# Weight loads behind a GpSimd gate, a second queue for the first small rows, and a mask in four selections, in a fused attention and tanh-shrink MLP kernel

## The chip, the cores and the metric

The kernel runs on one core of a Trainium2 chip. The metric is the time of one execution on the device in microseconds (us). Of the kernel before, three timed executions are given (median 357.6 us, 356.88 to 357.86) and one profiled execution, from which every duration below is taken.

## The reference

For 8 batches of 8 heads (sequence 576, head size 64) two attentions are added: a full one over q, k and v averaged in groups of four positions, whose result is repeated four times, and a local one in which a position sees only the positions less than four away. The sum, with the heads side by side, is x of 4608 tokens by 512. The output is (h - tanh(h)) @ w_out with h = x @ w_in.

```python
q_d, k_d, v_d = (t.reshape(B, H, Sd, 4, D).mean(axis=3) for t in (q, k, v))
out_up = np.repeat(sm_attn(q_d, k_d, v_d), 4, axis=2)
mask = np.abs(pos[:, None] - pos[None, :]) < 4
out_local = softmax(where(mask, scale * q @ k.T, -1e9)) @ v
x = (out_up + out_local).transpose(0, 2, 1, 3).reshape(B * S, H * D)
h = x @ w_in                       # 4608x512 @ 512x2048
out = (h - np.tanh(h)) @ w_out     # 4608x2048 @ 2048x512
```

## The kernel before

**The work.** Attention goes by pairs of heads: 32 pairs, four to a batch. Pair p belongs to batch p // 4, and its place in the batch is j = p % 4. Its inputs are K and Q rows (tile `st`, two transfers of 256 KB, L305), V rows (tile `vst`, two transfers of 160 KB, L329, the second holding the second head) and, once per batch, the last rows of K and Q that do not fit in 128 partitions (tile `sr`, four transfers of 64 KB, L318). K and Q are cast (L430, small rows L422), transposed on TensorE in the first 12 pairs (L453, L440) and copied back (L456, L444, L480, L485/L486 for the K side). Scores are L518, L526 and L532, exponentials L537, L541 and L545, the mask multiply L559. V is cast to `vw` (L360), its pooled form is a TensorE product (L391) copied out at L396. L572 multiplies the exponentials with V, L587 and L589 normalise, L614/L615 transpose back, L619 copies one piece, and L607 (`join`) writes the pair's 128 rows of `xT`.

**The dense part.** Tokens go in 9 blocks of 512. `mm1` (L645) multiplies `w_in` with `xT` into 16 pieces of 128 features, L658 takes the tanh, L661 the difference into `gT`; `mm2` (L671) multiplies `gT` with `w_out`; L685 copies and L696 stores. Block 0 needs the four pairs of batch 0, block 1 those of batches 0 and 1. Piece fc of `mm1` reads part fc // 4 of `w_in`; `mm2` goes through the four parts of `w_out` in turn for each 128 tokens.

**The weights.** Both matrices are loaded once, in four parts each, by DMAs that GpSimd issues (`load_w`, L345 and L349) and that cast float32 to bf16: 512 KB written for each part. They lie in a queue of their own; all other loads are issued by SyncE.

**The order.** No engine picks its work at run time. A planner (`Plan.order`, L58) goes through the operations with a cost and a priority for each, gives every engine the operation that can start first and, among those that could, the one of the lowest `pri`, and writes out one fixed order for each engine. An engine then works through its order and waits wherever an operand is not there. DMA is planned as one further lane, in which the transfers of all queues follow each other: 1000 ns for 256 KB of K or Q, 940 ns for 160 KB of V, 3100 ns for a part of the weights. Where the planned order leaves TensorE a gap of over 350 ns before the first `mm1` of block 1, `emit` writes matmuls on a zero tile into three quarters of it (`filler`, L799, L801 in the profile). The planner lets a weight load be issued once the *issue* of some V load has been planned (`("q", after)`); on the chip nothing makes it wait.

**Start.** GpSimd fills the constants (`c_mask` L284 with ten selections at L291 and L294), clears two tiles `v4` for later pairs (L744) and then reaches the weight loads. SyncE issues the small rows of batch 0 first, then K, Q and V pair by pair.

Of the kernel before, what the change touches and what calls it, by code (L numbers as in the profile page):

```python
# [7 lines left out]
FP32 = mybir.dt.float32  # L8
# [6 lines left out]
class Plan:  # L15
# [3 lines left out]

    LAT = {"PE": 270, "ACT": 160, "DVE": 130, "POOL": 160, "SP": 50, "DMA": 1900}

    def __init__(self):
        self.ops = []
# [32 lines left out]
    def order(self):  # L58
        ops, n = self.ops, len(self.ops)
        users = [[] for _ in range(n)]  # L60
        left = [0] * n
        for i, o in enumerate(ops):
            left[i] = len(o["deps"])
            for d in o["deps"]:
                users[d].append(i)
        at = [o["after"] for o in ops]
        free, ready = {}, {}
        start, engine = [None] * n, [None] * n
        pending = {k: len(v) for k, v in self.users.items()}
        ends = {}  # L70
        bank_free = [0.0] * 8
        held = [None] * 8
        port_free = 0.0
        self.held = []

        def make_ready(i):
            for eng in ops[i]["alts"]:
                ready.setdefault(eng, []).append(i)

        def bank_time(i):  # L80
            o = ops[i]["opens"]
            if not o:
                return 0.0, None
            best = (float("inf"), None)
            for c in o[1]:
                if any(held[b] is not None for b in c):
                    continue
                t = max(bank_free[b] for b in c)
                if t < best[0]:
                    best = (t, c)  # L90
            return best
        for i in range(n):
            if left[i] == 0:
                make_ready(i)
        for _ in range(n):
            best = None
            for eng, cand in ready.items():
                if not cand:
                    continue
                fr = free.get(eng, 0.0)  # L100
                if eng == "DMA":
                    i = min(cand, key=lambda i: (at[i], i))
                    now = max(fr, at[i])
                else:
                    now, i = None, None
                    eff = []
                    for c in cand:
                        t = max(at[c], bank_time(c)[0], fr)
                        if ops[c]["alts"][eng][3]:
                            t = max(t, port_free)  # L110
                        eff.append((t, c))
                    now = min(eff)[0]
                    if now == float("inf"):
                        continue
                    i = min((ops[c]["pri"], c) for t, c in eff if t <= now)[1]
                if best is None or now < best[0]:
                    best = (now, eng, i)
            if best is None:
                raise RuntimeError(f"no operation can be put next: {[(e, [(ops[c].get('what'), at[c], ops[c]['opens']) for c in cs[:6]]) for e, cs in ready.items()]} {held}")
            now, eng, i = best  # L120
            for other in ops[i]["alts"]:
                ready[other].remove(i)
            o = ops[i]
            _, ns, fn, port = o["alts"][eng]
            o["fn"], o["ns"] = fn, ns
            if o["opens"]:
                name = o["opens"][0]
                c = bank_time(i)[1]
                self.place[name] = c
                for b in c:  # L130
                    held[b] = name
                self.held.append([name, c, now, None])
            start[i], engine[i] = now, eng
            end = now + ns
            free[eng] = end
            if port:
                port_free = end
            for name in o["names"]:
                ends[name] = max(ends.get(name, 0.0), end + self.LAT[eng])
                pending[name] -= 1  # L140
                if pending[name] == 0:
                    for b in self.place[name]:
                        held[b] = None
                        bank_free[b] = ends[name]
                    for h in self.held:
                        if h[0] == name:
                            h[3] = ends[name]
            for u in users[i]:
                same = eng in ops[u]["alts"] and len(ops[u]["alts"]) == 1 and eng != "DMA"
                at[u] = max(at[u], end if same else end + self.LAT[eng] + ops[u]["slack"])  # L150
                left[u] -= 1
                if left[u] == 0:
                    make_ready(u)
        self.start, self.engine = start, engine
        return sorted(range(n), key=lambda i: (start[i], i))
# [22 lines left out]
def kernel(  # L178
# [9 lines left out]
    nc = tc.nc  # L188
# [3 lines left out]
    NP = H // 2  # L192
# [6 lines left out]
    STEP = 112  # L199
# [17 lines left out]
    def fixed(name, shape, dt, n=None, pool=const):  # L217
        if n is None:
            return pool.tile(shape, dt, name=name, tag=name)
        return [pool.tile(shape, dt, name=f"{name}{i}", tag=f"{name}{i}")  # L220
                for i in range(n)]

    NST, NVST, NVW, NV4 = 4, 5, 4, 2
    ident = fixed("ident", [128, 128], BF16)
    group = fixed("group", [128, 32], BF16)
    pick = fixed("pick", [128, 6, 128], BF16)
# [56 lines left out]

    def c_mask():  # L284
        GP.memset(mask, 1.0)
        parts = []
        for t in range(NT):
            parts.append((mask[:, COL[t]:COL[t] + 4 * NG[t]].rearrange(
                "p (c g) -> p c g", c=4), NG[t], STEP * t - 4 * G0[t]))
        for part, n, d in parts:  # L290
            GP.affine_select(  # L291
                out=part, in_=part, compare_op=ALU.is_ge, fill=0.0,
                base=d + 3, pattern=[[-1, 4], [-4, n]], channel_multiplier=1)
            GP.affine_select(  # L294
                out=part, in_=part, compare_op=ALU.is_ge, fill=0.0,
                base=3 - d, pattern=[[1, 4], [4, n]], channel_multiplier=-1)

    def load(ns, fn, keys, cost, pri, after=0.0):
        op("SP", ns, fn, writes=list(keys) + [("q", keys[0])], pri=pri, after=after)
        op("DMA", cost, None, reads=[("q", keys[0])], writes=keys, pri=pri)  # L300

    def load_qk(p):
# [7 lines left out]
    def load_rest(b):  # L310

        s = b % 2
        for n, src in enumerate((k, q)):
            for hh in range(2):
                base = src[b, hh]

                def issue(n=n, hh=hh, base=base):
                    nc.sync.dma_start(out=sr[s][n::2, hh, :], in_=bass.AP(  # L318
                        tensor=base.tensor, offset=base.offset + 512 * D,
                        ap=[[4 * D, 16], [2 * S * D, NP], [1, 4 * D]]))  # L320
                load(450, issue, [("sr", s, n, hh)], 260, 40 * b - 3000 - 4)

    def load_v(p):
        b, j, s = p // NP, p % NP, p % NVST
# [17 lines left out]
    def load_w(src, dst, name, f, after):  # L342
        def issue():
            if src is moe_w_in:
                GP.dma_start(out=dst[:, :, 512 * f:512 * f + 512],  # L345
                             in_=src[:, 512 * f:512 * f + 512].rearrange(
                                 "(c p) f -> p c f", p=128))
            else:
                GP.dma_start(out=dst[:, 4 * f:4 * f + 4, :],  # L349
                             in_=src.rearrange("(f p) n -> p f n", p=128)  # L350
                             [:, 4 * f:4 * f + 4, :])
        op("POOL", 1000, issue, reads=[("q", after)],
           writes=[(name, f), ("wq", name, f)], pri=-5000)
        op("DMA", 3100, None, reads=[("wq", name, f)], writes=[(name, f)], pri=-30)

    def prep_v(p):
        s, w = p % NVST, p % NVW
# [384 lines left out]
           pri=-9940)  # L742
    for i in range(NV4):
        op("POOL", 900, lambda i=i: GP.memset(v4[i], 0.0),  # L744
           writes=[("v4", i, 0), ("v4", i, 1)], pri=-20, port=True)

    load_qk(0)
    load_rest(0)
# [2 lines left out]
            load_qk(p + 1)  # L751
        load_v(p)
    for f in range(4):
        load_w(moe_w_in, w_in_sb, "w_in", f, ("vst", (2 + f) % NVST if f < 2 else 3, 1))
    nl = [NP]

    def load_next():
        if nl[0] < NPAIR:
            if nl[0] % NP == 0:
                load_rest(nl[0] // NP)  # L760
            load_qk(nl[0])
            load_v(nl[0])
            nl[0] += 1
        if 0 <= nl[0] - NP - 1 < 4:
            load_w(moe_w_out, w_out_sb, "w_out", nl[0] - NP - 1,
                   ("vst", (nl[0] - 1) % NVST, 1))

    work = [attention(p) for p in range(NPAIR)]
    for a in work:
# [63 lines left out]
```

## Time and profile before

| | |
|---|---|
| median of 3 executions | 357.6 us (356.88 to 357.86) |
| profiled execution: its own time | 358.21 us |
| profiled execution: span, first to last instruction | 356.5 us |
| mean granted TensorE clock | 0.966 |
| TensorE busy | 329.3 us (92%) |
| VectorE, ScalarE, GpSimd busy | 221.3, 225.2, 129.7 us |
| weights' queue (software dynamic) | 4224 packets, 4.19 MB |
| all other loads, stores, transposes (hardware dynamic) | 97824 packets, 50.61 MB |

The page gives busy time by engine over the span, then the span in 40 slices of 8.9 us with one digit per engine (tenths of the slice). A busy TensorE is not a TensorE at its best: filler matmuls count as busy, and the granted clock stands in a row of its own. The chain of waits is followed back from the last instruction; the timeline of one engine lists its instructions with the idle time ahead of them and what ended it. A DMA's issue (SPq, POOL) and its landing are two things: the issue is the time on the issuing engine.

### The profile page before, as it was taken

What the parts mean: (1) busy time and instruction counts of PE and PEld (TensorE: products, weight loads), DVE (VectorE), ACT (ScalarE), POOL (GpSimd) and SP (SyncE); (2) the same over time, 40 slices, a digit from 0 to 9 for tenths busy, and PEclk for the clock granted to TensorE, in tenths of its full rate; (3) what the DMA queues carried; (4) which work ended last, traced back from release to release, by engine and by line L of the source; (5) the groups of instructions that cost most, each with busy time, mean ns of one, the idle gap of its engine ahead of it and who ended that gap; (6) DMA issues with size and microseconds to landing.
All of it is one profiled execution on the core that took longest, in us unless ns stands there. A gap on an engine that the chain in (4) does not pass through costs nothing.

```text
span 356.5 us, 7044 instructions
## 1 busy us (share of the span) xinstructions
PE 329.3 (92%) x2574; PEld 169.1 (47%) x2621; DVE 221.3 (62%) x409; ACT 225.2 (63%) x396; POOL 129.7 (36%) x161
## 2 busy tenths in 40 slices
PE   5826699999999999999999999999999999999994
PEld 2414355555554544554454444545555444444441
DVE  3715378756897487868959875788686533444300
ACT  3525378666987477578967886898787344444411
POOL 8303323153433331744929557548441000000000
PEclk9855899999999999999999999999999999999999
DMA  5999997848998916999699978723510211111031
GB/s 155 239 208 222 263 254 217 225 112 185 243 242 203 262 46 149 212 265 266 154 239 253 223 207 230 190 71 94 121 31 2 59 30 33 40 48 31 29 88 60
DMA packets 102083, 55.26 MB, mean 155 GB/s; under 512 B 69152, under 2 KB 97440, under 8 KB 102048
## 3 DMA queue, kind: packets, MB, share of 16 engines
q1 hardware_dynamic: 97824, 50.61, 56.5%
q0 software_dynamic: 4224, 4.19, 7.0%
q8 instruction: 20, 0.33, 0.4%
q14 instruction: 15, 0.12, 0.1%
HBM read 43.65 MB, written 9.44 MB: 149 GB/s over the span
## 4 chain that ended last, share of the span: by engine, by line
PE 83%; issue 1%; ACT 1%; DVE 1%; ACTq 0%
PE ps L671 35%; PE ps L645 34%; PE ps L572 4%; PE ps L614 3%; PE ps L518 2%; PE ps L526 1%; PE ps L453 1%; PE ps L532 1%; PE ps L391 1%; PE ps L615 0%; ACT kt L485 0%; ACT kq L456 0%; ACT y L685 0%; DVE xT L607 0%; DVE half L495 0%
## 5 line engine op out<-in xcount | busy, mean ns | idle before, releaser
L645 PE MATMUL ps<-xT,w_in_sb 128*128 128x512 bf16 x552 | 140.3, 382 | 2.0 <-issue 0.6
L671 PE MATMUL ps<-w_out_sb,gT 128*128 128x512 bf16 x557 | 139.3, 379 | 1.5 <-issue 0.8
L661 DVE TENSOR_TENSOR gT<-ps,u 128x512 bf16<-128x512 f32 x144 | 97.7, 687 | 54.3 <-ACT u L658 52.6
L658 ACT ACTIVATE u<-ps 128x512 f32<-128x512 f32 x144 | 85.8, 599 | 48.8 <-PE ps L645 45.7
L645 PEld LDWEIGHTS <-w_in_sb 128*128 128x128 bf16 x576 | 53.0, 98 | 59.5 <-issue 1.8
L671 PEld LDWEIGHTS <-gT 128*128 128x128 bf16 x576 | 52.6, 98 | 56.5
L495 POOL TENSOR_TENSOR half<-kq 128x576 f32<-128x576 bf16 x22 | 29.9, 1358 | 41.1 <-DVE kq L480 20.5
L559 DVE TENSOR_TENSOR E<-E,mask 128x1152 bf16<-128x1152 bf16 x32 | 27.9, 871 | 18.8 <-ACT E L541 18.8
L537 ACT ACTIVATE E<-ps 128x912 bf16<-128x912 f32 x32 | 29.8, 932 | 8.8 <-PE ps L518 6.0
L685 ACT COPY y<-ps 128x512 f32<-128x512 f32 x36 | 21.1, 585 | 17.2 <-PE ps L671 17.0
L430 POOL CAST qr<-st 128x512 bf16<-128x512 f32 x37 | 24.1, 661 | 21.1 <-DMA st<-in_k_dram 17.3
L377 POOL TENSOR_TENSOR vp<-v 128x256 bf16<-128x256 f32 x20 | 14.6, 731 | 46.8 <-PE ps L572 46.4
L589 DVE TENSOR_TENSOR ln<-ps,r 128x768 bf16<-128x768 f32 x32 | 30.6, 956 | 1.1 <-DVE r L587 0.2
L485 ACT COPY kt<-kq 128x576 bf16<-128x576 bf16 x22 | 26.0, 1181 | 2.4 <-DVE kq L480 2.2
L373 POOL TENSOR_TENSOR v<-v 128x512 f32<-128x512 f32 x20 | 26.2, 1312 | 1.0
L572 PEld LDWEIGHTS <-E 128*128 128x128 bf16 x576 | 22.3, 99 | 8.1 <-DVE E L559 1.1
L360 ACT CAST vw<-vst 128x640 bf16<-128x640 f32 x21 | 15.3, 731 | 14.8 <-DMA vst<-in_v_dram 7.5
L607 DVE TENSOR_TENSOR xT<-ps,od 128x336 bf16<-128x336 bf16 x64 | 16.5, 300 | 12.1 <-ACT od L619 12.1
L545 ACT ACTIVATE E<-ps 128x576 bf16<-128x576 f32 x32 | 20.9, 653 | 0.0
L572 PE MATMUL ps<-vw,E 128*128 128x65 bf16 x320 | 19.5, 195 | 0.7 <-DVE E L559 0.5
L500 POOL TENSOR_TENSOR qkd<-half 128x288 bf16<-128x288 f32 x17 | 14.0, 825 | 16.3 <-PE ps L572 8.5
L572 PE MATMUL ps<-vp,E 128*128 128x65 bf16 x256 | 18.3, 195 | 0.0
(64 smaller groups left out, 264.0 us busy)
## 6 DMA issues: line engine op xcount, KB each, us to landing
vst<-in_v_dram SPq DMA_DIRECT2D x64, 160.0 KB, 4.1
st<-in_k_dram SPq DMA_DIRECT2D x32, 256.0 KB, 3.9
st<-in_q_dram SPq DMA_DIRECT2D x32, 256.0 KB, 4.0
v<-in_v_dram SPq DMA_DIRECT2D x20, 256.0 KB, 3.6
w_in_sb<-in_moe_w_in_dram POOLq DMA_DIRECT2D x4, 512.0 KB, 12.4
w_out_sb<-in_moe_w_out_dram POOLq DMA_DIRECT2D x4, 512.0 KB, 16.1
out_dram<-y SPq DMA_DIRECT2D x8, 256.0 KB, 3.1
out_dram<-y SPq DMA_DIRECT2D x8, 224.0 KB, 2.6
```

The costliest lines, as they stand in the source:

```text
L373: eng.tensor_tensor(out=v2, in0=v4[s][:, :, :, 0:128], in1=v4[s][:, :, :, 128:256], op=ALU.add)
L430: (eng, ns, lambda dst=dst, src=src, fn=fn: fn(out=dst, in_=src), port)
L485: ("ACT", 1180, lambda: A.copy(out=ktv, in_=src), False),
L495: eng.tensor_tensor(out=half, in0=flat[:, 0:576], in1=flat[:, 576:1152], op=ALU.add)
L537: A.activation(out=E[s][:, :, E0:E0 + 456], in_=at(s1)[:, :, PS0:512], func=AF.Exp, scale=SCALE)
L559: op("DVE", 760, lambda: V.tensor_tensor(out=el, in0=el, in1=mask.unsqueeze(1).to_broadcast([128, 2, S]), op=ALU.mult), reads=["mask"], wr ...
L572: T.matmul(po[:, hh, 65 * n:65 * n + 65], E[s][:, hh, e:e + 128], vv, start=start, stop=stop)
L589: op("DVE", 960, lambda: V.tensor_tensor(out=ln[s].rearrange("p n (h d) -> p h n d", d=D), in0=blocks()[:, :, :, 0:64], in1=r[s].unsqueeze ...
L645: T.matmul(at(name)[:, 0, :], w_in_sb[:, dc, fc * 128:(fc + 1) * 128], xT[dc][:, kb * 512:kb * 512 + 512], start=(dc == 0), stop=(dc == N_ ...
L658: op("ACT", 600, lambda: A.activation(out=u[us], in_=at(name)[:, 0, :], func=AF.Tanh), reads=[("hd", kb, fc)], writes=[("u", us)], pri=-1, ...
L661: op("DVE", 690, lambda: V.tensor_tensor(out=gT[g][:, fc, :], in0=at(name)[:, 0, :], in1=u[us], op=ALU.subtract), reads=[("hd", kb, fc), ( ...
L671: T.matmul(at(name)[:, 0, :], gT[g][:, fc, ts * 128:ts * 128 + 128], w_out_sb[:, fc, :], start=(fc == 0), stop=(fc == N_FF - 1))
```

## The change

Four things are edited.

1. **A gate ahead of the weights.** Before the first `w_in` part GpSimd copies one element of the second V tile of pair 2 (`vst[2]`) into a one-element tile `gate`. The copy can run only when that transfer has landed, and since GpSimd works in order, all eight weight loads are issued after it. The four `w_out` loads are queued together when pair 4 is loaded, not one for each pair. In the planner the weights get a DMA lane of their own, `DW`, with 6200 ns for a part, and a transfer of the other lane takes up to twice its cost while `DW` is occupied.
2. **Small rows of batch 0** are issued by ScalarE, not by SyncE.
3. **The mask** is made by four selections over three or two column groups at once, not by ten over one.
4. **The clearing of `v4`** gets priority 75 in the planner, not -20.

```diff
@@ Plan.order @@
-                if eng == "DMA":
+                if eng in ("DMA", "DW"):
...
+            if eng == "DMA":
+
+                ns += min(ns, max(0.0, free.get("DW", 0.0) - now))
             end = now + ns
@@ c_mask @@
-        for part, n, d in parts:
+        for part, n, m, d, e in (
+                (mask[:, 0:336].rearrange("p (t c g) -> p t c g", t=3, c=4), 3, 28, -8, 0),
+                (mask[:, 336:576].rearrange("p (t c g) -> p t c g", t=2, c=4), 2, 30, 0, -8)):
             GP.affine_select(
                 out=part, in_=part, compare_op=ALU.is_ge, fill=0.0,
-                base=d + 3, pattern=[[-1, 4], [-4, n]], channel_multiplier=1)
+                base=d + 3, pattern=[[e, n], [-1, 4], [-4, m]], channel_multiplier=1)
...
@@ load_rest @@
-                    nc.sync.dma_start(out=sr[s][n::2, hh, :], in_=bass.AP(
+                    (nc.scalar if b == 0 else nc.sync).dma_start(out=sr[s][n::2, hh, :], in_=bass.AP(
...
-                load(450, issue, [("sr", s, n, hh)], 260, 40 * b - 3000 - 4)
+                load(450, issue, [("sr", s, n, hh)], 260, 40 * b - 3000 - 4,
+                     eng="ACT" if b == 0 else "SP")
@@ load_w @@
-        op("POOL", 1000, issue, reads=[("q", after)],
-           writes=[(name, f), ("wq", name, f)], pri=-5000)
-        op("DMA", 3100, None, reads=[("wq", name, f)], writes=[(name, f)], pri=-30)
+        if after:
+            op("POOL", 110, lambda: GP.tensor_copy(out=gate, in_=vst[after[1]][0:1, 1, 4, 0:1]),
+               reads=[after], writes=["gate"], pri=-5001, port=True)
+        op("POOL", 760, issue, reads=["gate"], writes=[(name, f), ("wq", name, f)], pri=-5000)
+        op("DW", 6200, None, reads=[("wq", name, f)], writes=[(name, f)], pri=-30)
@@ start @@
         op("POOL", 900, lambda i=i: GP.memset(v4[i], 0.0),
-           writes=[("v4", i, 0), ("v4", i, 1)], pri=-20, port=True)
+           writes=[("v4", i, 0), ("v4", i, 1)], pri=75, port=True)
...
-        load_w(moe_w_in, w_in_sb, "w_in", f, ("vst", (2 + f) % NVST if f < 2 else 3, 1))
+        load_w(moe_w_in, w_in_sb, "w_in", f, ("vst", 2, 1) if f == 0 else None)
@@ load_next @@
-        if 0 <= nl[0] - NP - 1 < 4:
-            load_w(moe_w_out, w_out_sb, "w_out", nl[0] - NP - 1,
-                   ("vst", (nl[0] - 1) % NVST, 1))
+        if nl[0] == NP + 1:
+            for f in range(4):
+                load_w(moe_w_out, w_out_sb, "w_out", f, None)
```

## The prediction

> **What bounds the kernel now.** I read the page's slices first, then the chain of waits, then the timelines of the engines over the first 60 us, then the DMA queues by window.
>
> ```profile
> PE   5826699999999999999999999999999999999994
> PEclk9855899999999999999999999999999999999999
> DMA  5999997848998916999699978723510211111031
> ```
>
> From the sixth slice on (after some 46 us) TensorE is full. The windows view gives 295.95 us busy in 52 to 352 us, so 4 us idle in 300; what happens there can't give much. Ahead of that the slices are poor, the clock is at half, and DMA is full from the second slice on. The chain can be followed back no further than
>
> ```profile
> 487 pieces in order of time: start us, us, what
> ...
> 45.97 1.01 PE ps L645 x4
> ```
>
> so the last 310 us are TensorE's work one after the other, and the time is the moment at which the dense part starts in earnest, plus that. Up to 46 us an engine waits for a transfer: pair 2's V holds ScalarE and TensorE, pair 3's K and V hold GpSimd.
>
> ```profile
> 26.00 0.73 ACT L360 CAST vw<-vst 128x640 bf16<-128x640 f32 x1 [6.62 <-DMA vst<-in_v_dram]
> ...
> 26.78 0.80 PE L391 MATMUL ps<-vw,pick 128*128 128x128 bf16 x6 [6.21 <-ACT vw L360]
> ...
> 28.23 0.61 POOL L430 CAST qr<-st 128x512 bf16<-128x512 f32 x1 [15.77 <-DMA st<-in_k_dram]
> ...
> 38.21 0.72 POOL L360 CAST vw<-vst 128x640 bf16<-128x640 f32 x1 [6.64 <-DMA vst<-in_v_dram]
> ...
> 47.96 0.52 DVE L607 TENSOR_TENSOR xT<-ps,od 128x336 bf16<-128x336 bf16 x2 [1.01 <-ACT od L619]
> ```
>
> The last line is pair 3's `join`, which block 0 needs: 10.3 us from V landing (38.2) to its end (48.5). Why the V rows come late is in the issues and in the queues from 18 to 24 us:
>
> ```profile
> 7.49 3.13 POOL L345 DMA_DIRECT2D w_in_sb<-in_moe_w_in_dram  x4
> 10.59 1.87 POOL L349 DMA_DIRECT2D w_out_sb<-in_moe_w_out_dram  x2
> ...
> 9.56 1.42 SPq L329 DMA_DIRECT2D vst<-in_v_dram  x2
> ...
> q0 software_dynamic: 931, 0.93, 90.8%
> q1 hardware_dynamic: 929, 0.23, 29.7%
> ```
>
> Columns of the last two: packets, MB, share of 16 engines. The two queues pass as many packets (931 and 929), but a weight packet is 1 KB and a V packet 256 bytes: V gets 0.04 MB/us (0.23 MB in 6 us). Pair 2's second V transfer takes 15.7 us from issue to landing. The weights' queue is active from 10.1 to 41.5 us: 31.4 us, 3.9 us a part.
>
> **The change part by part.** *The gate.* Ahead of V of pair 2 lie 2.8 MB (three pairs of 832 KB, small rows 256 KB). Without weights the queues moved 289 GB/s in 5 to 10 us and 261 in 42 to 57 us: 10 to 11 us from the first data at 2.2 us, so V of pair 2 lands at 12 to 13.5 us instead of 25.9; I take 13. Behind it on the same queue are pair 3's K and Q (0.52 MB, 1.9 us: 15 instead of 28 and 30 us). The first weight packet came 2.6 us after its issue began (7.49 to 10.1), so weights run from 13 + 2.6 = 15.6 to 47 us. Of pair 3's 1280 V packets some 740 are through by then; the other 540 go at the weights' rate of 4224 packets in 31.4 us, 134 per us, and take 4 us: landed at 19.6 us instead of 38.2. With the measured 10.3 us to the `join`, and 2 to 3 us because pairs 0 to 3 now come close together on VectorE, `xT` of batch 0 is complete at 32 to 33 us instead of 48.5. `w_in` parts land at 3.9 us intervals from 19.5 to 31.3 us, in time; `w_out` is there by 47 us, and its first use (65.4 us now, some 50 after) still finds it. Cap of the gain: 15 us.
>
> The copy of one element has no row; the nearest are memsets of one element per partition (0.10 us) and the V cast (0.72 us): 0.1 taken. Queued behind the waiting copy on GpSimd are the eight issues and then casts and sums of pairs 3 and on. Today GpSimd waits from 12.5 to 28.2 us anyway, so the wait until 13 us costs nothing; were the cover gone, pair 3's cast would wait for the eight issues. These cost 8 x 0.82 us (3.13 + 1.87 us for six) = 6.6 us, to 19.6 us. More than six issues in one go are not shown: from nothing to waiting for the first part (19.5 us) and another; I take nothing, as the sixth took 1.1 us at most.
>
> The Trainium skill speaks against queueing them there: by "SBUF — State Buffer", sections "SBUF: two separate sides" and "A bandwidth-pool intuition that's wrong", VectorE's two-port operations keep GpSimd from writing descriptors, and a load of 0.62 us becomes one of 3.1 us. By the page the eight could take up to 25 us, an estimate, and the sum would lose most of its gain. The row says 0.75 to 1.13 us for the issues between 7.5 and 12.5 us, with VectorE busy in half of that time, and I go by it.
>
> *What becomes late next.* The weights are as many as before and now lie over batch 1. Packet for packet: small rows 256, then per pair 256 + 256 + 2 x 640 = 1792. To the end of V of pair 5 that is 540 + 256 + 3584 = 4380, at 134 per us 32.6 us: about 46 to 48 us, when the weights end; from rates by bytes (pair 3 with the second small rows, 14.6 us, and 12.2 us for a pair) 44 us. I take 46. Now it lands at 46.6 to 47.3 us, no later; but TensorE reaches its product (L391) only here:
>
> ```profile
> 59.26 0.52 PE L391 MATMUL ps<-vw,pick 128*128 128x128 bf16 x6
> ```
>
> With 0.7 us for the cast and 0.5 us to the product it can run at 47 us, 12.3 us earlier. How much of block 0 stands ahead of it in the new order is not in the trace. Before, it was 10 of 16 pieces of 0.86 us. If the planner leaves ten there too, the gain is 12.3 us; if none, 12.3 - 8.6 = 3.7 us. Its lanes make pair 5's V due some 7 us earlier than before (weights no longer in the same lane), so nearer the middle: five pieces, 12.3 - 4.3 = 8 us. Pairs 6 and 7 come after the weights at full rate, 3 us a pair, by 53 us, and TensorE has 13.8 us of `mm2` of block 0 for that time. From there on the order is as full as before, and the gain is kept.
>
> *ScalarE's issues.* The four small transfers took SyncE 1.33 + 1.23 us; all later loads go out 2.6 us sooner, which is in the 12 to 13.5 above (DMA was 21% busy in the first 5 us). No issue by ScalarE is shown; SyncE's and GpSimd's rows give 0.6 to 0.8 us, so 2.5 to 3 us in all, beside ScalarE's wait until 5.12 us; without that cover they'd cost 3 us once.
>
> *Mask and clearing.* Ten selections ran from 2.60 to 5.76 us, 3.2 us. Four of 336 and 240 columns: by the rows of 32 (0.21) and 120 columns (0.30) some 1 ns a column, 0.52 and 0.42 each, 1.9 us in all; bounds 1.2 and 3.2. The mask's first reader is at 15.17 us, and GpSimd then waits for the gate: nothing. The clearing (1.84 us) likely stays where it is, since GpSimd has nothing else ready; later it would cost 1.84 us on an engine that is busy 36% of the time: nothing.
>
> **Sum.** The profiled execution's own time is 358.2 us (span 356.5), 0.6 above the median. 358.2 - 8 = 350.2; less 0.6: **349.6 us**.
>
> **The rivals.** *A, the whole lead is kept* (15%): pair 5 stands behind enough of block 0, and only pair 3's lead counts: 13 to 15 us, 344. For it: V of pair 5 lands no later than today. Against it: an order written out in advance, with TensorE waiting at each place.
>
> *B, batch 1 takes the lead back* (19%): product of pair 5 ahead of nearly all of block 0, its V at 48 us or later, perhaps also pair 6's cast on ScalarE ahead of the tanh: gain below 4 us, 354 to 358.7, a third of it within the limit of measurement. For it: 0.04 MB/us for V under the weights. That the change does nothing is in here too: if V of pair 2 landed so late that the gate costs what it brings. Against it: the bytes in the queue ahead of it.
>
> *C, slower: the planner reckons the weights too dear* (16%). With 8 x 6200 ns = 49.6 us for what the chip did in 31.4 us, the last part of `w_out` is due near 67 us in the order and there near 48 us. Between the parts TensorE has 3.5 us of `mm2` for 6.2 us, so gaps of up to 2.7 us, into which `emit` writes filler matmuls that then have to be run, and attention is put ahead of `mm2`. Against: pairs 4 to 7 have about 8 us of TensorE work for these gaps. It ends slower than before once fillers and misplaced work cost over 8 us: 37 matmuls of 0.216 us on top of the 41 weight loads of L801 now. At 12 us: 361 us.
>
> **How the numbers follow.** The likeliest case (50%) is a gain of 4 to 12.5 us, 345 to 353.5 us, at 349.6. The range 342.5 to 359 takes in A's greater part and B, and leaves out C and the end of A, just under 2 in 10. A measurement of this kernel can tell about 0.3%, 1.1 us, from no change: faster 0.50 + 0.15 + 0.13 = 0.78, same 0.06, slower 0.16.
>
> **What would show it.** Right: V cast of pair 2 (L360) at 13 to 15 us with no wait of 6 us; eight weight issues in one row from about 13 us; the weights' queue active to about 47 us; pair 3's `join` (L607) at 32 to 34 us; the chain traceable to before 40 us; the product of pair 5 waiting for DMA to about 47 us, with `mm1` pieces ahead of it; 52 us and on as full as now. Wrong: weight issues of 2 us and more, GpSimd held after the sixth issue, the third V landing after 18 us, more than 60 filler matmuls after 30 us, or new idle time of TensorE beyond 60 us.

## The result and the profile after

| | before | after |
|---|---|---|
| median of 7 runs each, same chip | 357.72 us (356.88 to 358.43) | 355.65 us (354.5 to 356.34) |
| ratio, 95% interval | | 0.9941 (0.9921 to 0.996) |
| profiled execution: its own time, span | 358.21, 356.5 us | 356.3, 354.6 us |
| mean granted TensorE clock | 0.966 | 0.978 |

The change makes the kernel faster by 2.1 us, 0.6%. The forecast was 349.6 us, a gain of 8.

The page's slices of after; a slice is 8.9 us:

```profile
PE   6782679999999999989999999999999999999994
PEclk9997869999999999999999999999999999999998
DMA  8999998958959647999699987534401211111131
```

The DMA row is full from the second slice as before. TensorE does more in the third slice (8, before 2) and has its own hole now in the fourth and fifth (2 and 6), from 27 to 45 us, with the clock below full in the fourth to sixth (7, 8, 6). The chain of waits, first without a window and then in the window from 20 to 60 us:

```profile
473 pieces in order of time: start us, us, what
...
25.93 19.75 DMA vst<-in_v_dram
...
45.79 0.74 POOL vw L368
46.57 0.80 PE ps L399 x6
47.37 4.27 PE ps L653 x10
```

It can be followed into the transfer of pair 5's V, 19.75 us long, through its cast to its product on TensorE. (The line numbers are 8 higher than before in this region.) GpSimd's timeline shows the gate and both V casts:

```profile
13.42 0.31 POOL L359 COPY gate<-vst 1x1 f32<-1x1 f32 x1 [2.17 <-DMA vst<-in_v_dram]
13.68 3.15 POOL L351 DMA_DIRECT2D w_in_sb<-in_moe_w_in_dram  x4
16.80 3.20 POOL L355 DMA_DIRECT2D w_out_sb<-in_moe_w_out_dram  x4
...
33.10 0.72 POOL L368 CAST vw<-vst 128x640 bf16<-128x640 f32 x1 [10.55 <-DMA vst<-in_v_dram]
...
45.79 0.73 POOL L368 CAST vw<-vst 128x640 bf16<-128x640 f32 x1 [7.83 <-DMA vst<-in_v_dram]
```

The gate opens at 13.4 us and the eight issues go out back to back. V of pairs 4 (33.1) and 5 (45.8) comes late, as V of pairs 2 and 3 did before. TensorE's timeline:

```profile
33.88 0.80 PE L399 MATMUL ps<-vw,pick 128*128 128x128 bf16 x6 [6.55 <-POOL vw L368]
34.47 2.77 PE L653 MATMUL ps<-xT,w_in_sb 128*128 128x512 bf16 x6
37.03 0.85 PE L622 MATMUL ps<-ident,ln 128*128 128x128 bf16 x6
...
46.57 0.80 PE L399 MATMUL ps<-vw,pick 128*128 128x128 bf16 x6 [3.54 <-POOL vw L368]
47.17 4.47 PE L653 MATMUL ps<-xT,w_in_sb 128*128 128x512 bf16 x10
...
52.45 2.32 PE L653 MATMUL ps<-xT,w_in_sb 128*128 128x512 bf16 x10
...
155.11 0.51 PE L622 MATMUL ps<-ident,ln 128*128 128x128 bf16 x6 [1.32 <-DVE ln L597]
```

Three things are to be read here. TensorE waits 6.55 us for V of pair 4 while the back transposes of pair 3 (L622), on which block 0 depends, stand behind that product and start at 37.03 only. It waits 3.54 us more for V of pair 5. And the ten `mm1` matmuls behind that wait take 4.47 us where ten later ones take 2.32. The windows view (stretch, its length, busy us and count of PE, PEld, DVE, ACT and POOL, granted clock, DMA share, GB/s) gives the reason:

```profile
33.50:38.00 4.50, 4.12 (x23) 2.28 (x24) 0.00 (x0) 0.89 (x2) 2.96 (x4) 0.50 1.20 222
...
46.50:52.00 5.50, 5.43 (x24) 2.27 (x23) 1.38 (x2) 2.86 (x5) 5.07 (x8) 0.50 0.95 231
```

The granted clock is 0.50 in the stretch behind each wait.

**The lead.** To see where a gain comes and goes I count TensorE's useful work: every weight load with the time of its matmul at full clock (0.216 us at 512 columns, 0.056 at 128, 0.031 at 65, 0.040 at 112 to 144), fillers zero. The lead of a kernel at an amount of work is how much earlier than the kernel before it gets there. After the change it is 18 us when before is at 44 us, 6.4 us when before is at 53 us (there TensorE reaches pair 5's product), 4.0 at 61 us, the same at 99 us, 3.6 at 154 us and 2.0 from 163 us to the end. So about 16 of the 18 us are given back, in three steps: the wait for V of pair 5, the half clock behind it, and something at 155 us, where the timeline above has the wait for `ln` of batch 3. A lead is read from one profiled execution of each kernel.

### The profile page after: what moved, and what is told of

The parts are those of the page before. It is cut to its first block, busy times and chain, and to the rows that moved or that the text cites. A ratio compares the mean times of both kernels' runs of the same rounds, so it can differ in the third digit from the quotient of the medians.

```text
span 354.6 us, 7059 instructions
## 1 busy us (share of the span) xinstructions
PE 330.0 (93%) x2611; PEld 166.7 (47%) x2611; DVE 225.5 (64%) x407; ACT 223.0 (63%) x398; POOL 127.8 (36%) x156
## 3 DMA queue, kind: packets, MB, share of 16 engines
q0 software_dynamic: 4224, 4.19, 7.1%
## 4 chain that ended last, share of the span: by engine, by line
PE 85%; DMA 7%; DVE 3%; ACT 1%; SPq 1%; issue 1%; POOL 0%; ACTq 0%; POOLq 0%
PE ps L679 36%; PE ps L653 35%; DMA vst<-in_v_dram 6%; PE ps L580 4%; PE ps L622 3%; PE ps L526 2%; PE ps L534 1%; PE ps L540 1%; DMA sr<-in_k_dram 1%; DMA st<-in_k_dram 1%; DVE ln L597 1%; PE ps L399 1%; PE ps L461 1%; DVE qkd L508 1%; DVE half L503 1%
## 5 line engine op out<-in xcount | busy, mean ns | idle before, releaser
L653 PE MATMUL ps<-xT,w_in_sb 128*128 128x512 bf16 x576 | 146.1, 386 | 0.3 <-DVE xT L615 0.3
L679 PE MATMUL ps<-w_out_sb,gT 128*128 128x512 bf16 x576 | 143.4, 379 | 0.0
L653 PEld LDWEIGHTS <-w_in_sb 128*128 128x128 bf16 x576 | 53.9, 99 | 60.7 <-issue 3.9
L503 POOL TENSOR_TENSOR half<-kq 128x576 f32<-128x576 bf16 x19 | 26.0, 1367 | 36.7 <-ACT kq L488 22.4
L438 POOL CAST qr<-st 128x512 bf16<-128x512 f32 x39 | 26.9, 700 | 3.7 <-DMA st<-in_q_dram 1.4
L615 DVE TENSOR_TENSOR xT<-ps,od 128x336 bf16<-128x336 bf16 x64 | 16.5, 299 | 16.1 <-ACT od L627 16.1
L580 PEld LDWEIGHTS <-E 128*128 128x128 bf16 x576 | 21.6, 97 | 9.0 <-DVE E L567 3.0
L493 ACT COPY kt<-kq 128x576 bf16<-128x576 bf16 x20 | 23.6, 1181 | 0.8 <-DVE kq L464 0.5
L580 PE MATMUL ps<-vw,E 128*128 128x65 bf16 x320 | 19.0, 193 | 1.3 <-DVE E L567 1.3
L627 ACT COPY od<-ps 128x144 bf16<-128x144 bf16 x32 | 8.9, 279 | 15.4 <-PE ps L623 15.4
L622 PE MATMUL ps<-ident,ln 128*128 128x128 bf16 x192 | 16.3, 222 | 2.1 <-DVE ln L597 2.1
L368 POOL CAST vw<-vst 128x640 bf16<-128x640 f32 x12 | 8.7, 727 | 26.0 <-DMA vst<-in_v_dram 20.6
```

The lines of the kernel that those rows point to most:

```text
L438: (eng, ns, lambda dst=dst, src=src, fn=fn: fn(out=dst, in_=src), port)
L503: eng.tensor_tensor(out=half, in0=flat[:, 0:576], in1=flat[:, 576:1152], op=ALU.add)
L580: T.matmul(po[:, hh, 65 * n:65 * n + 65], E[s][:, hh, e:e + 128], vv, start=start, stop=stop)
L622: T.transpose(px[:, 128 * n:128 * n + 128], ln[s][:, n, :], ident)
L653: T.matmul(at(name)[:, 0, :], w_in_sb[:, dc, fc * 128:(fc + 1) * 128], xT[dc][:, kb * 512:kb * 512 + 512], start=(dc == 0), stop=(dc == N_ ...
L679: T.matmul(at(name)[:, 0, :], gT[g][:, fc, ts * 128:ts * 128 + 128], w_out_sb[:, fc, :], start=(fc == 0), stop=(fc == N_FF - 1))
```

## Experiments

My theory was that the planner's prices decide: beside the weights, it reckons 160 KB of V at twice 940 ns, 1880 ns, while the chip passes its 640 packets at one for each weight packet. At 31.4 us for 4224 packets (7.43 ns each) that is 4755 ns. An order made with too low a price puts the products of pairs 4 and 5 where their V isn't there yet. The main rival was the half clock behind the waits; two others were the third step at 155 us and the gate itself.

**The clock alone.** `warm` keeps the order of the change and puts 62 and 36 filler matmuls of 256 columns ahead of the products of pairs 4 and 5, into the waits.

```diff
+            for _ in range({4: 62, 5: 36}.get(p, 0)):
+                T.matmul(at(name)[:, 0, 256:512], warm[:, 0:128], warm[:, 0:256],
+                         start=True, stop=True)
```

> The changed kernel with the same order on every engine, and on TensorE alone filler matmuls of 256 columns ahead of the V products of pair 4 (62 of them) and pair 5 (36), in the same PSUM bank beside the product; they fill the two waits of 6.5 and 3.5 us. Theory 'clock' (the half granted clock after the waits costs about 1.5 us in 33 to 38 us and 2.5 us in 46.5 to 52 us, and is part of why the lead shrank): the ten mm1 matmuls that took 4.47 us take 2.2, V products still wait for DMA until 33 and 45.8 us, the lead at 60 us grows from 4 to some 6.5 us; at the end 1 to 2 us faster than the changed kernel if nothing else binds, the same if batch 3's last join binds. Rival 'V alone': the clock's share hides beside waits on other engines, the lead stays at 4 us, no change.

Measured: 353.79 us, ratio to before 0.9897 (0.985 to 0.9943), span 352.1, mean clock 0.999. Its TensorE timeline and the same window:

```profile
46.64 0.50 PE L402 MATMUL ps<-vw,pick 128*128 128x128 bf16 x6 [1.10 <-POOL vw L368]
46.98 2.32 PE L656 MATMUL ps<-xT,w_in_sb 128*128 128x512 bf16 x10
```

```profile
46.50:52.00 5.50, 5.36 (x41) 2.72 (x40) 2.53 (x6) 4.65 (x9) 5.19 (x8) 1.00 1.06 235
```

The product starts as late as in the change (46.64), but the ten matmuls behind it take 2.32 us at full clock. The lead at 61 us is 6.5, not 4.0, and stays 2.5 us higher to the end (4.5). In the profiled executions the half clock costs 2.5 us. The medians differ by 1.9 us, and the intervals of the two ratios overlap a little, so the size is known less well than the mechanism, which the ten matmuls show. It is not the main part of the loss.

**The prices.** `true_costs` leaves every instruction of the change as it is and gives the planner the measured prices: a weight part 31.4 / 8 us, and a transfer that lies beside weights 7.43 ns for each of its packets. `lane_3930` has only the first price, with the doubling kept; `packets_6200` only the second.

```diff
-                ns += min(ns, max(0.0, free.get("DW", 0.0) - now))
+                both = max(0.0, free.get("DW", 0.0) - now)
+                slow = 7.43 * o["packets"]
+                if slow > ns:
+                    ns = slow if slow <= both else both + ns * (1.0 - both / slow)
...
+           packets={"st": 256, "vst": 640, "sr": 64}.get(keys[0][0], 0))
...
-        op("DW", 6200, None, reads=[("wq", name, f)], writes=[(name, f)], pri=-30)
+        op("DW", 3930, None, reads=[("wq", name, f)], writes=[(name, f)], pri=-30)
```

> The changed kernel with only the planner's costs set to what the trace showed: 3930 ns for a part of the weights, and for a transfer beside them 7.43 ns times its packets (256 for K or Q, 640 for V, 64 for small rows). Transfers and gate are untouched; only the order follows. Theory 'order' (the order puts the V products of pairs 4 and 5 too early, and block 0's mm1, whose inputs are there from 33 us on, behind them): pair 3's join moves from 38.9 to 32 to 34 us, TensorE works on block 0 while V of pairs 4 and 5 is under way, the lead at 60 us grows from 4 to 7 to 9 us. Rival 'data' (whatever the order, TensorE has too little to do until V of pairs 4 and 5 is there): the lead at 60 us stays at 4 to 5 us. In both cases the end time also depends on when batch 3's last join comes; if that binds, the time stays within 1.5 us of the changed kernel's 355.6.

> The changed kernel with one number of the planner altered: a part of the weights costs 3930 ns (measured) and not 6200; a transfer beside it still at most doubles, so V of pair 4 and 5 is still reckoned early (V beside weights takes some five times its cost). Transfers and gate untouched. If the 6200 alone was what spoiled the order (batch 3's attention due late because the lanes are overbooked, mm2 spread out): 343 to 347. If the price of V beside the weights is what matters (products of pairs 4 and 5 put ahead of block 0): TensorE waits again 5 to 7 us near 27 to 34 us and 3 us near 46 us, lead at 60 us some 4 to 7 us, and 349 to 354.

> The measured prices for transfers beside the weights (7.43 ns a packet), but the change's 6200 ns for a part of the weights: the fourth corner beside the changed kernel (355.6: 6200 and doubling), 3930 with doubling (353.8) and 3930 with packets (343.4). With 6200 the planner thinks that weights last 49.6 us and so that V crawls until 66 us: pairs 5 to 7 are due late, block 1 and batch 3 with them. If both prices must be right: block 0 is early (lead near 15 us at 40 us), then TensorE's order runs out of work or attention of batches 1 and 3 comes late, the lead falls, and the time is 349 to 358. If the price by packets is all that counts: 343 to 346.

Measured: `true_costs` 343.35 us, ratio 0.9594 (0.955 to 0.9639), span 341.6: 12.3 us faster than the change by the medians. `lane_3930` 353.79 us, 0.988 (0.9842 to 0.9918); `packets_6200` 351.78 us, 0.9798 (0.976 to 0.9836). GpSimd's and TensorE's timelines of `true_costs`:

```profile
46.11 0.72 POOL L372 CAST vw<-vst 128x640 bf16<-128x640 f32 x1 [5.17 <-DMA vst<-in_v_dram]
```

```profile
33.70 0.50 PE L403 MATMUL ps<-vw,pick 128*128 128x128 bf16 x6 [1.34 <-POOL vw L372]
...
46.89 0.51 PE L403 MATMUL ps<-vw,pick 128*128 128x128 bf16 x6 [1.04 <-POOL vw L372]
```

V of pair 5 is cast at 46.11, not earlier than in the change (45.79): the transfers are the same. What differs is what stands ahead of its product. The view by source line counts the `mm1` matmuls that start before that product, in the change and in `true_costs`:

```profile
L653 PE MATMUL ps<-xT,w_in_sb x18: 376/379/634, 22.6 to 42.7; 128*128 128x512 bf16 x18
```

```profile
L657 PE MATMUL ps<-xT,w_in_sb x54: 376/379/391, 20.9 to 45.2; 128*128 128x512 bf16 x54
```

18 against 54, and 7.8 us is what 36 more are worth at 0.216. The waits shrink to 1.34 and 1.04 us, the clock stays up over them (no slice of its page is below 9), and there is no wait at batch 3's `join`. The lead is 17.2 us when before is at 53 us, 16.5 at 61 us, where 7 to 9 had been expected, and 14.9 at the end. With `lane_3930` the waits come back (5.07 us ahead of pair 4's product, 4.79 ahead of pair 5's) and the lead is some 4 us from there on. With `packets_6200` the order holds through pair 5 (lead 16.5 us at 53 us) and the lead then falls to 8.2 at 99 us and 5.3 at the end. So in this planner both prices are needed: the packet price for the V rows, the part's price for what comes behind.

**The gate with other orders.** `true_no_gate` keeps the measured prices and the small edits and issues the weights as before, without the gate. `gate_alone` is the kernel before, with its planner (only the issue of a part is priced 760 ns, not 1000), and the gate with all eight loads behind it.

```diff
# true_no_gate: true_costs, and
-        if after:
-            op("POOL", 110, lambda: GP.tensor_copy(out=gate, ...
-        op("POOL", 760, issue, reads=["gate"], ...
+        op("POOL", 760, issue, reads=[("q", after)], ...
# gate_alone: before, with the gate copy and the w_out loads together, still
         op("DMA", 3100, None, reads=[("wq", name, f)], writes=[(name, f)], pri=-30)
```

> The kernel with the planner's measured costs, the small edits of the change, but no gate: weights are issued by GpSimd as before, behind the issue of V loads only. If the gate is worth something once the order is honest: V of pair 2 lands near 25 and of pair 3 near 37 us as in the kernel before, batch 0 is complete at 45 to 48 us, and the time is 355 to 360, 12 us or more behind the gated kernel with the same costs (343.4). If the honest order alone was worth the 14 us: 343 to 348.

> The kernel before with the gate and nothing else: planner costs, lanes, small rows, mask and clearing as before. The transfers then run much like the changed kernel's (weights from some 17 to 48 us). If the change's own planner lane (6200, doubling) helped the order: slower than the changed kernel's 355.6 by 2 us or more. If the gate brought the gain and the lane nothing: 354 to 356.5.

Measured: `true_no_gate` 353.85 us, 0.9881 (0.9841 to 0.9922), between the two expectations; `gate_alone` 366.19 us, 1.0198 (1.0124 to 1.0272), slower. From the kernel before, measured prices and small edits without a gate bring about 1.2% and a gate without prices costs 2%; together they bring 4.1%. TensorE's timeline of `gate_alone` has the longest wait of all kernels here:

```profile
48.89 0.29 PE L456 MATMUL ps<-ident,qr 128*128 128x128 bf16 x1 [7.30 <-POOL qr L433]
```

There the planner still has all transfers in one lane, and a K cast that waits 12.55 us for its transfer on GpSimd stands ahead of TensorE.

**The step at 155 us.** Batch 3 (pairs 12 to 15) is the first whose K and Q are transposed by DMA. `ne16` has TensorE transpose these pairs too. `second_gate` puts `w_out` behind a second gate, V of pair 5, and `second_ne16` does both; `true_second` and `true_second_ne16` do the same with the measured prices.

```diff
# second gate
-        if nl[0] == NP + 1:
+        if nl[0] == NP + 2:
             for f in range(4):
-                load_w(moe_w_out, w_out_sb, "w_out", f, None)
+                load_w(moe_w_out, w_out_sb, "w_out", f, ("vst", 0, 1) if f == 0 else None)
# ne16
-    NE, NBK = 12, 32
+    NE, NBK = 16, 32
```

> The changed kernel with batch 3's K and Q transposed by TensorE and not by DMA, all else as in the change. TensorE gets 3.2 us more work. If the last 2 us of the changed kernel's lead (4 us until 152 us, 2 after) fall to batch 3's last join: the join comes before 150 us, no wait there, and the time is the changed kernel's 355.6 less 2 plus 3.2: 356 to 357.5. If the loss has another cause: 358 to 360 (3.2 us of work on top), or below 355.

> The changed kernel with a second gate: the four w_out loads wait, by the same kind of one-element copy, for V of pair 5, and only the four w_in loads for V of pair 2. The planner's costs are those of the change, so the order changes too. Theory 'data': w_in is through at 31 us, V of pair 4 lands at 28 to 31 instead of 33, V of pair 5 at 33 to 36 instead of 45.8 us; the second wait of TensorE (3.5 us) and the half clock after it go, w_out lands at 50 to 53 us, in time for mm2 at 60; the lead at 60 us is 7 to 9 us. Rival 'order': V lands so early but the products wait elsewhere and the lead stays near 4 us; or w_out comes too late and TensorE waits at mm2.

> The kernel with the second gate (354.2, lead 10 us at 116 us of work, cut to 4.5 by TensorE's wait for batch 3's last join near 150 us), with batch 3's K and Q transposed by TensorE like those of batches 0 to 2 and not by DMA, which is more TensorE work: 4 x (0.45 + 0.34) us = 3.2 us. If batch 3's attention, and not the ramp, is the second bound: its last join comes earlier than TensorE needs it, the lead of 10 us is kept but for the 3.2 us, and the time is 349 to 352. If the wait only moves to a later batch: 354 to 358.

> Measured costs and the second gate (w_out behind V of pair 5). If batch 1's V still bounds the start (TensorE waits 1.3 us at 33.7 and 1.0 us at 46.9 us with one gate, and block 0 fills the rest): 1 to 3 us faster than 343.4. If block 0's work hides these rows anyway: the same within 1.5 us, or slower where w_out comes late for mm2.

> Measured costs, second gate, and batch 3 transposed by TensorE. The kernel with measured costs and second gate had a lead of 17 us until 137 us and 11 after TensorE's wait for batch 3's last join (345.4 us). If that join is the bound: the 17 us are kept but for 3.2 us of added TensorE work, 341 to 343. If another wait takes its place: 345 to 349.

| | median us | ratio to before | lead at 99, 154, 163 us, end |
|---|---|---|---|
| ne16 | 356.66 | 0.9958 (0.9921 to 0.9994) | 5.0, 4.8, 5.0, 5.2 |
| second_gate | 354.22 | 0.9898 (0.9855 to 0.9942) | 10.0, 9.5, 4.8, 4.0 |
| second_ne16 | 349.59 | 0.9763 (0.9712 to 0.9815) | 12.0, 11.5, 12.0, 11.9 |
| true_second | 345.41 | 0.9622 (0.9583 to 0.9661) | 17.6, 17.2, 11.2, 11.6 |
| true_second_ne16 | 344.79 | 0.9605 (0.9536 to 0.9674) | 17.1, 16.1, 16.7, 16.6 |

(With 16 pairs on TensorE there are some 3 us more of useful work, so a lead of 5 there is a gain of about 2.) What TensorE waited for between 130 and 160 us, in `second_gate` and in `true_second` (us in total, times, longest):

```profile
PE ps L535 <- DVE xT L616: 1.9, 2, 1.7
PE ps L623 <- DVE ln L598: 1.3, 1, 1.3
PE ps L527 <- ACT kt L494: 0.9, 1, 0.9
```

```profile
PE ps L539 <- DVE xT L620: 2.0, 1, 2.0
PE ps L627 <- DVE ln L602: 1.3, 1, 1.3
```

In both kernels the lead drops by 5 to 6 us just there, and in the kernels with 16 pairs on TensorE neither wait nor drop is left. The waits alone are 4.1 and 3.3 us. The rest is the half clock again, as the windows behind the waits show, first of `second_gate`, then of `true_second`:

```profile
152.10:155.40 3.30, 2.90 (x12) 1.12 (x13) 1.11 (x3) 1.43 (x3) 0.00 (x0) 0.51 0.86 234
```

```profile
143.80:150.50 6.70, 5.91 (x24) 2.40 (x25) 2.88 (x6) 2.53 (x6) 2.17 (x3) 0.51 1.15 222
```

Twelve `mm1` matmuls take 4.02 and 5.30 us there, and 2.75 us a little later in `true_second`. In the change the clock stays at 1.00 over its shorter wait. What the wait for `ln` is, VectorE's timeline of the change shows:

```profile
153.83 0.23 DVE L595 RECIPROCAL r<-ps 128x12 f32<-128x12 f32 x1 [1.02 <-PE ps L580]
154.09 0.96 DVE L597 TENSOR_TENSOR ln<-ps,r 128x768 bf16<-128x768 f32 x1
```

Behind the last product (L580) come the reciprocal and `ln`, and then TensorE transposes it back at 155.11. The order has nothing for TensorE to do in between, and it waits for just this chain. It waits 1.32 us each time: at 155.1 us in the change, at 148.9 in `second_gate`, at 141.6 in `true_second`. So it isn't tied to a moment, it goes with the order: in all three the 192 `mm1` and 192 `mm2` matmuls of blocks 0 to 2 are behind it, so TensorE has no dense work left that doesn't need batch 3. With TensorE transposing pairs 12 to 15 the planner writes another order, without it; but so it does in `true_costs`, with 12 pairs. Why batch 3 stands late in one order and not in the other stays open. As to what was expected: `ne16` and `second_ne16` came as they should if batch 3 binds. With the measured prices both missed: `true_second` has 17.6 us of lead at 99 us, 2.7 more than `true_costs`, but loses 6 at batch 3 and is not 1 to 3 us faster; `true_second_ne16` loses nothing there, but has the 3 us more work and took 344.79 us for 341 to 343. `second_gate` also shows a way that needs no better price: its lead at 53 us is 11.4 us, since V of pair 5 lands before `w_out` takes its share.

**The small edits.** `gate_and_lane` is the change with the three other edits undone (small rows by SyncE, ten selections, the clearing's priority); `true_small_undone` is `true_costs` with the same undone.

```diff
-   (nc.scalar if b == 0 else nc.sync).dma_start(out=sr...
+   nc.sync.dma_start(out=sr...
-   writes=[("v4", i, 0), ("v4", i, 1)], pri=75, port=True)
+   writes=[("v4", i, 0), ("v4", i, 1)], pri=-20, port=True)
...
```

> The changed kernel with the three small edits taken back: small rows of batch 0 by SyncE, ten selections for the mask, priority -20 for the clearing; gate and planner lane stay. If ScalarE's issue carries its 2.6 us into the ramp: V of pair 2 lands at 15 to 16 instead of 13.4 us, weights are active from 18 to 48, V of pair 5 lands near 48, and the lead at 60 us is some 2 us smaller, the time 357 to 358. If that lead is lost on the way (batch 3's last join binds): the same as the changed kernel, 355 to 356.

> Gate and measured costs, with the three small edits taken back (small rows by SyncE, ten selections, clearing at -20). If ScalarE's issue saves its 2.6 us on the path now that the order follows the transfers: V of pair 2 at 16 instead of 13.6 us, everything after it 2 to 3 us later, 345.5 to 347. If not: 342 to 344.5.

Measured: 355.77 us, 0.9914 (0.9878 to 0.995), no different from the change by the intervals; and 347.0 us, 0.9675 (0.9612 to 0.9737), 3.7 us above `true_costs` by the medians and 2.9 by the ratios, close to what was expected. The gate opens at 17.67 and 17.65 us without the small edits and at 13.4 to 13.7 with them. Only 1.6 and 1.8 us of that are V of pair 2 landing later (14.93 for 13.37, 15.39 for 13.58 us); in both kernels a sum stands ahead of the copy on GpSimd and waits for VectorE. With the measured prices most of the 4 us arrive in the time. With the change's prices they don't, and why isn't shown: `gate_and_lane` has 6.5 us of lead at 61 us, where the change has 4.0 and less had been expected, and 3.2 at the end.

**Another queue for V.** `true_v_scalar` is `true_costs` with batch 1's V issued by ScalarE, so that three queues share the engines.

```diff
-   nc.sync.dma_start(out=vst[s][:, i]...
+   (nc.scalar if b == 1 else nc.sync).dma_start(out=vst[s][:, i]...
```

> Measured costs, and V of pairs 4 to 7 issued by ScalarE, so that they lie in a third queue beside K and Q (SyncE) and the weights. If the queues take turns packet by packet (931 against 929 packets in 18 to 24 us), V of pair 5 lands some 8 us sooner, near 38 instead of 46 us, and the weights end some 5 us later than 46 us. In the time, at most 1 to 2 us either way, since block 0 hides V now; ScalarE gives 8 x 0.63 = 5 us of issuing in its in-order queue, which could cost up to 3 us. Rival: the hardware queues share one turn, and V of pair 5 lands near 46 us as before.

Measured: 351.78 us, 0.9793 (0.9749 to 0.9838), 8.4 us slower than `true_costs` by the medians, 7 by the ratios. ScalarE's queue from 14 to 20 us, all three queues from 24 to 30 us (packets, MB, share), and a line each of ScalarE's and TensorE's timelines:

```profile
q10 hardware_dynamic: 1312, 0.33, 29.7%
```

```profile
q0 software_dynamic: 681, 0.68, 66.9%
q1 hardware_dynamic: 644, 0.60, 37.4%
q10 hardware_dynamic: 628, 0.16, 12.9%
```

```profile
37.96 0.76 ACT L373 CAST vw<-vst 128x640 bf16<-128x640 f32 x1
```

```profile
30.52 0.59 PE L814 MATMUL ps<-lT 128*128 128x512 bf16 x1 [5.96 <-ACT E L550]
```

The queues take nearly equal turns. But V of pair 5 did not land near 38 us, as expected: ScalarE issued it at 12.05 us already, its 1280 packets passed from 14 to 20 us, and it landed at 19.72 us, ahead of the weights' main part (45.99 in `true_costs`). Its cast at 37.96 us waited for ScalarE's order and not for data. The price is at the start: V of pair 2 lands at 14.99 us (13.58), the gate opens at 18.79 us, ScalarE, whose V issues stand among its casts and exponentials, waits 6.84 us, by the profile for small rows, and TensorE stands for 5.96 us until 30.5. The lead is 5.6 us when before is at 44 us (17.5 in `true_costs`) and 6 at the end. The earlier V buys nothing. How much of this is ScalarE's issuing and how much the new order, no run separates.

A caution holds for all runs but `warm`: a changed price or edit rewrites the whole order, so differences of 2 to 4 us between two of these kernels can be the order's chance. The 12 us of `true_costs` and the 10 us between it and `true_no_gate` are well beyond that, and all four kernels with the gate, both measured prices and V on SyncE lie at 343 to 347 us, while no other kernel here is below 349.

## Why the prediction was right and wrong

**Right: the start.** V of pair 2 lands at about 13 us, as taken; the copy takes 0.31 us, not 0.1. The eight issues take 3.15 + 3.20 = 6.35 us (6.6 predicted), and neither the seventh nor the eighth waits. The 3.1 us a load that the Trainium skill, "SBUF — State Buffer", section "A bandwidth-pool intuition that's wrong", gives beside a VectorE copy did not show: 0.79 us each, with VectorE 4.88 of 5 us busy from 15 to 20 us. The weights' queue is active from 15.64 to 45.6 us (15.6 to 47). V of pair 3 landed at 16.38 us, 3 us ahead of the 19.6 reckoned, since its first transfer was in at 15.72 us, when the weights had just begun. That its cast ran at 19.17 us is ScalarE's order, and the agreement with 19.6 luck. The four selections take 0.43 to 0.55 us each and run from 2.61 to 4.69 us, 2.08 in all (1.9), the clearing stays in its place, and ScalarE's issues (2.52 us) lie beside a wait.

**Right: what becomes late.** V of pair 5 landed at 45.67 us (46; before 46.74, a little ahead of the 46.6 to 47.3 that the prediction read), and its product ran at 46.57 (47), 12.7 us earlier than before (12.3). Packets decided it, as reckoned: 926 of the weights and 927 of the other queue from 24 to 30 us. The Trainium skill, "DMA: Bandwidth & Descriptors", section "Queues, rings and completion order", says that each DMA engine goes round-robin between the queues it has work for, at packet granularity; the counts agree, with two queues and with three (681, 644, 628).

**Wrong: `xT` of batch 0 at 32 to 33 us.** It was complete at 38.85 us (48.5 before). I had looked for a wait of TensorE at pair 5's product only. Pair 4's, with a wait of 6.55 us, stands ahead of pair 3's back transposes. That this cost the end little by itself, because the wait for pair 5 came behind it anyway, is argued and not shown by a run.

**Close: how much of block 0 stands ahead of pair 5's product.** I took five pieces of 16 from the middle between ten and none; it was 18 matmuls, 4.5 pieces. Before, it was 42 by the weight loads that start ahead of the product (39 matmuls are in the trace, which lacks a few records):

```profile
L645 PEld LDWEIGHTS <-w_in_sb x42: 95/98/147, 34.8 to 58.4; 128*128 128x128 bf16 x42
```

That gives 12.7 - 24 x 0.216 = 7.5 us, so the term that was most in doubt was nearly right. The product is reached ahead of a little attention work too, 0.7 us of it: 6.8 us, and the lead there is 6.4.

**The step that failed: "From there on the order is as full as before, and the gain is kept."** 8 us were to be kept from pair 5's product to the end; 6.4 were there and 2.1 were left. Of the 6.4 us, 2.4 go to the half clock by 61 us, shown by `warm`, which holds the clock and keeps 2.5 us more; the prediction had no term for the clock behind a wait. Two more go by 163 us, 1.6 of them from 154 us on, at the wait for batch 3's `ln` (1.32 us), which the order of before doesn't have. (The 0.33 us for its `xT` are no loss: before waits 0.37 us for that at 158.85 us.) 6.4 - 2.4 - 2.0 = 2.0 us. I had read "295.95 us busy" as proof that nothing in the dense part could give or take much. But that full stretch belonged to the order of before; the change has the planner write another one, with a gap of its own at 155 us.

**The rivals.** The time fell into rival B's band, a gain below 4 us, but not by B's way: V landed where I had put it, and 4.5 pieces stood ahead of pair 5's product, as the likeliest case had it; the gain was lost behind that product. Rival A, the whole lead kept at 344 us, is what `true_costs` gives, 343.35 us, by an order alone. For C, the planner's prices, I had looked at the weights' price, too dear, and counted fillers. They became fewer (31 weight loads of the filler line, 41 before). C's price does cost time, though not by fillers and only once V is priced right: 7 to 8 us between `packets_6200` and `true_costs`. The wrong price that I had not looked at was that of V beside the weights, 1880 ns for 4755, too cheap. The prediction had both numbers, 134 packets a microsecond and 640 packets, and did not hold them against the planner's doubling; that comparison would have pointed at the V products of pairs 4 and 5 standing ahead of their data.

## What to carry to other kernels

Where an order is written ahead of time, a change that moves transfers is worth what the planner's prices for them are worth: reprice each transfer beside its new neighbour, in packets if queues take turns by the packet, before judging the change. Removing a wait at the start gives a lead, and the lead has to be followed to the end: a rewritten order can give part of it back 100 us later, and a dense stretch in the profile of before says nothing about that. And a wait has a tail: an idle TensorE runs on at half clock for some microseconds, which cheap matmuls in the wait avoid.

## What was not expected of the hardware

- The granted clock falls to 0.50 at 31.5 us, 4.2 us after TensorE's last matmul before the wait, and is full again at 38.3, 4.4 us after work went on; the second time it falls at 45.1 us, 2.1 us after the last matmul, and is full again at 52.0, after 5.4 us of work. The Trainium skill, "TensorE: Matmul & The Clock Gate", Part 1, gives a window of about 3.4 us for both directions and says that it is free-running. The trace agrees: the four changes lie 6.83 us apart, two such windows, so a delay counted from the last matmul need not be 3.4 us. A window need not be idle throughout: in the 3.41 us that ended at 45.1 us TensorE worked for 1.19 us and the clock fell, and in the next 3.41 us it worked for 1.99 us and the clock stayed down.
- Fillers of 256 columns in the waits were enough to hold it: 1.00 in the same window.
- With three queues active the packets split in three nearly equal parts, and batch 1's V, issued early on a queue of its own, landed up to 26 us earlier (pair 5 at 19.72 for 45.99 us); the kernel was slower all the same.
